# One equality table of 256 columns for both direct slots of a routed expert layer

## The chip, the cores and the metric

The kernel runs on one core of a Trainium2 chip. The metric is the device time of one launch in microseconds, lower is better. The engines are TensorE (PE: matrix products), VectorE (DVE), ScalarE (ACT), GpSimd (POOL) and SyncE (SP, which here only issues DMAs). Each runs its own list of instructions in order, and semaphores tie the lists together.

## The reference, cut to what matters

Attention (two sequences, 8 heads), then a soft expert layer, then a layer in which every one of 1536 tokens goes to its two best of eight experts. The change lies in the last of these:

```python
noisy_logits = x @ w_gate + np.log1p(np.exp(x @ w_noise)) * noise
top2 = np.argpartition(-noisy_logits, 2, axis=1)[:, :2]
top2_l = np.take_along_axis(noisy_logits, top2, axis=1)
top2_l = top2_l - top2_l.max(-1, keepdims=True)
top2_w = np.exp(top2_l)
top2_w /= top2_w.sum(-1, keepdims=True) + 1e-09
for e in range(E):
    for k in range(2):
        mask = top2[:, k] == e
        h = np.maximum(x[mask] @ w1[e], 0.0)
        out[mask] += top2_w[mask, k, None] * (h @ w2[e])
```

## The kernel before

It has three stages in one program: attention (to about 106 us of the profile), the soft expert layer, whose eight experts' weights stream in until about 141 us, and the routed layer, called the second experts here. The output of the soft layer is never written out per token: a token's row is a combination `c` of 32 slot outputs, so for the routed layer a token is 32 numbers, split in two fp16 parts and laid out as 128 columns of `crow` (line 633).

*Routing.* With the logits of all tokens in 12 groups of 128, VectorE finds each token's two best experts (lines 936 to 940), forms a mask, and TensorE counts by products with triangular matrices (952 to 959) where in its expert a token stands. From the running position `plc` come a slot number and a row inside the slot: a slot is a block of 128 tokens of one expert. Each expert owns 3 slots (`OWN`), 24 slots in all, and one further slot shares the overflow.

*Slots.* A slot is worked on in three steps: its tokens' columns are brought to `ct` (128 columns by 128 tokens), `slot_h` (line 1103) multiplies them with the expert's first weights `Gst` (already combined with the soft layer's outputs) and ScalarE and VectorE (`slot_l`, 1118) leave the rectified result in two fp16 parts, and `slot_y` (1208) makes the 24 products with the second weights `w2hl`, high part first. The result is scaled and added to the output by an indirect DMA.

*Where the columns come from.* For slots 2 and on from DRAM: GpSimd completes `crow` by the gates (`gates_a`, 1145), SyncE writes it to the DRAM table `ctab` (1152), and GpSimd gathers 128 rows per slot (`slot_a`, 1250) by the indices `gidx`, which TensorE sums out of one-hot tables (`ids`, 1198); TensorE transposes them (`slot_t`, 1012). That takes long, so slots 0 and 1, both of expert 0, go directly: `placed` (1137) compares, for each of the 12 groups, the token's key with 128 places and so writes an equality table `z` of 128 columns, and `direct` (1125) sums the products of `crow` with it, 12 products per slot. Slot 0 has its own table and so does slot 1, with all keys shifted by 2. 

*The second weights.* Expert by expert ("rank" in the code, class `Rank`, 771) fp32 weights are loaded, their largest value gives a power of two (`pow2_a` on TensorE, 753, `pow2_b` on VectorE, 760), and they are split in a high part (`w_hi`, ScalarE) and a remainder (`w_lo`, VectorE, line 811). `K0`, `K1`, `K2` are the first three ranks.

*What sets the order.* From the routed layer on, the order on PE, DVE, ACT and POOL is written out by hand: what is written first is issued first. `warm(k)` issues k products whose results nobody reads; `next(y0)` issues two of the 24 products of slot 0. SyncE restarts the weight loads only when it has read a flag `go` that GpSimd sets behind the first two gathers (1404, 1405).

*Helper tables.* `exp24`, `rows6` and `slot6` are constants, spread out by one copy each (line 929): the first by ScalarE, the other two by GpSimd.

The two lines that the change turns around most, as they were:

```python
        for t, a, by in ((exp24, K24, nc.scalar.copy), (rows6, 361, nc.gpsimd.tensor_copy), (slot6, KSLOT, nc.gpsimd.tensor_copy)):
        ...
            for t in range(a, b):
                nc.vector.tensor_scalar(z[:, t], places, keys[:, k, t:t + 1], None, ALU.is_equal)
```

Of the kernel before, what the change touches and what calls it, by code (L numbers as in the profile page):

```python
# [19 lines left out]
NT = 12  # L20
# [32 lines left out]
KSLOT = 489  # L53
# [6 lines left out]
def emit(tc, d, near=True, stop=None):  # L60
    nc = tc.nc
    es = ExitStack()
    with es:
# [696 lines left out]
        def pow2_b(px, a, b):  # L760
# [10 lines left out]
        class Rank:  # L771
# [20 lines left out]
            def w_pow_b(self):  # L792
                (self.sw, self.iw), = pow2_b(self.pw, 1, 2)
# [133 lines left out]
        for t, a, by in ((exp24, K24, nc.scalar.copy), (rows6, 361, nc.gpsimd.tensor_copy), (slot6, KSLOT, nc.gpsimd.tensor_copy)):  # L927
            n, m = t.shape[1], t.shape[2]
            by(t, k16[:, a:a + n].unsqueeze(2).to_broadcast([128, n, m]))
        K0.w_abs(0)  # L930
        K0.g_pow_a()
        warm(12)
# [27 lines left out]
        warm(3)  # L960
# [4 lines left out]
        K0.w_abs(3)  # L965
        pst = ph_([128, 2, 256]), ps_y.tile([128, 2, 256], F32, name="y")
# [158 lines left out]
        def direct(z):  # L1125
            pct = pm_([128, 128])
            for t in range(NT):
                nc.tensor.matmul(pct, crow[:, t, 0:128], z[:, t], start=(t == 0),
                                 stop=(t == NT - 1))
            return pct  # L1130

        def direct_t(pct):
            ct = wk3.tile([128, 128], F16, name="ct")
            nc.vector.tensor_copy(ct, pct)
            return ct

        def placed(z, k, a, b):
            for t in range(a, b):
                nc.vector.tensor_scalar(z[:, t], places, keys[:, k, t:t + 1], None, ALU.is_equal)

        places = k16[:, 361:489]
# [3 lines left out]
        def gates_a():  # L1145
# [6 lines left out]
            nc.sync.dma_start(out=ctab.rearrange("(p t) c -> p t c", p=128), in_=crow.bitcast(F32))  # L1152

        z0, z1 = [scratch([128, NT, 128], F16) for _ in range(2)]
        placed(z0, 0, 0, NT)
        K0.w_scale_a()
        pct0 = direct(z0)
        K0.w_pow_a()
        ttt(e2, m8[:, :, 1], m8[:, :, 0], ALU.subtract)
        nc.scalar.activation(e2, e2, AF.Exp)  # L1160
        nc.gpsimd.tensor_scalar(gts[:, 0], e2, 1.0, 1e-9, ALU.add, ALU.add)
        nc.vector.tensor_reduce(cnt8, pcnt.rearrange("p (e t) -> p e t", e=8), AX.X, ALU.add)
        t0 = direct_t(pct0)
# [11 lines left out]
        placed(z1, 1, 0, NT)  # L1175
# [6 lines left out]
        pct1 = direct(z1)  # L1182
        K1.g_scale_a()
# [3 lines left out]
        t = direct_t(pct1)  # L1187
        slot_l(*h0, (0,))
# [19 lines left out]
        def slot_y(j, hh):  # L1208
# [16 lines left out]
            ys = ((z0, z1)[j].rearrange("p t c -> p (t c)")[:, 0:1024].bitcast(F32) if j < 2 else wk3.tile([128, 512], F32, name="ys", bufs=2) if j % 3 else  # L1225
# [449 lines left out]
```

## Time and profile before

| | |
|---|---|
| time, median of 3 runs (lowest to highest) | 342.07 us (340.68 to 342.35) |
| the profiled execution's own time | 341.8 us |
| its span | 340.0 us |
| TensorE busy | 315.6 us, 93% of the span |
| VectorE, ScalarE, GpSimd busy | 200.3, 207.9, 139.5 us |
| mean granted TensorE clock | 0.98 |
| moved by DMA | 89.22 MB, 262 GB/s over the span |

The span is what the profiler saw, from the first to the last instruction; the time lies 1.8 us above it. The chain of work that ended last is of no help here, since it breaks off at the last branch of the program; the stretches of time and the waits of each engine are read instead. Names in the profile are those of tiles: most small tiles of the routing lie in one buffer and so are called `w2hl`, `k` is the table of constants, `c` on TensorE's reading side is `crow` or a constant, and `h`, `y`, `m`, `pg` are PSUM buffers. A timeline row merges neighbours that look alike and gives their number as xN, with the time from the first start to the last end.

### The profile page before, as it was taken

The numbers are of one execution on the slowest core, as the hardware profiler recorded it, in microseconds if no ns is written. First come the engines' busy times: TensorE is split into PE (matmuls) and PEld (weight loads), VectorE is DVE, ScalarE is ACT, GpSimd is POOL, SyncE is SP. The second block draws the span as 40 slices with busy tenths as digits, with TensorE's granted clock in tenths as the row PEclk, the third lists the DMA queues.
The fourth block names the chain that finished last, engine by engine and source line by source line (L and its number), as shares of the span: only waits on it lengthen the run. The fifth ranks groups of instructions, "written<-read, shape, count | busy, mean of one in ns | idle before, by whom it ended". The sixth has DMA issues, their size and how long they took to land. (4 is left out here: it accounts for less than half of the span.)

```text
span 340.0 us, 7478 instructions
## 1 busy us (share of the span) xinstructions
PE 315.6 (93%) x2691; PEld 187.7 (55%) x2691; DVE 200.3 (59%) x715; ACT 207.9 (61%) x489; POOL 139.5 (41%) x194
## 2 busy tenths in 40 slices
PE   8999999999978899977889999999999999999990
PEld 3789878888855444334554454545454545544540
DVE  2755655556526200089877685797669396898110
ACT  2788868777822211096658787496878695876320
POOL 4366543645610000122155583554653535533131
PEclk9999999999979999998799999999999999999998
DMA  6999999999999999999917999949999955222542
GB/s 178 295 329 290 316 315 313 310 271 344 339 398 400 396 394 394 393 400 393 377 33 159 300 321 362 318 105 322 299 301 291 326 179 72 35 33 32 63 63 38
DMA packets 49291, 89.22 MB, mean 262 GB/s; under 512 B 3408, under 2 KB 18384, under 8 KB 49248
## 3 DMA queue, kind: packets, MB, share of 16 engines
q1 hardware_dynamic: 44848, 81.20, 71.7%
q0 software_dynamic: 4400, 7.48, 14.1%
q8 instruction: 23, 0.38, 0.4%
q14 instruction: 20, 0.16, 0.2%
HBM read 78.53 MB, written 10.14 MB: 261 GB/s over the span
## 5 line engine op out<-in xcount | busy, mean ns | idle before, releaser
L1219 PE MATMUL y<-w2hl,hh 128*128 128x512 f16 x552 | 125.3, 379 | 0.8 <-ACT w2hl L1230 0.8
L1219 PEld LDWEIGHTS <-hh 128*128 128x128 f16 x552 | 52.5, 98 | 62.0 <-issue 4.0
L216 ACT ACTIVATE Tt<-Tt,nm 128x167 f32<-128x167 f32 x96 | 40.5, 424 | 12.9 <-DVE nm L209 12.0
L1120 DVE SCALAR_TENSOR_TENSOR hh<-h,hh 128x512 f16<-128x512 f32 x46 | 29.6, 685 | 23.0 <-ACT hh L1112 22.9
L1234 POOL DMA_INDIRECT out_y<-ys,sidx x15 | 26.9, 1794 | 27.2 <-ACT ys L1228 14.1
L811 DVE SCALAR_TENSOR_TENSOR w2hl<-w,pm,w2hl 128x1024 f16<-128x1024 f32 x28 | 35.0, 1279 | 1.2 <-issue 0.7
L231 POOL TENSOR_TENSOR Pb<-Tt,r 128x668 f32<-128x668 f32 x24 | 31.2, 1299 | 9.4 <-DVE r L223 9.1
L209 DVE CUSTOM_DVE_ANT_0 Tt<-s,bias 128x167 f32<-128x167 f32 x96 | 26.3, 328 | 14.1 <-PE s L206 14.0
L1252 POOL DMA_INDIRECT cT<-ctab,gidx x25 | 30.3, 1214 | 8.5 <-issue 4.9
L1112 ACT ACTIVATE hh<-h 128x512 f16<-128x512 f32 x46 | 25.0, 597 | 14.0 <-PE h L1111 14.0
L206 PE MATMUL s<-kx,qd 128*128 128x167 f32 x192 | 31.6, 307 | 0.4 <-DVE nm L209 0.2
L808 ACT ACTIVATE w2hl<-w,pm 128x1024 f16<-128x1024 f32 x28 | 31.4, 1150 | 0.0
L243 ACT ACTIVATE PT<-pt 128x512 f32<-128x512 f32 (+1 forms) x48 | 24.4, 558 | 10.4 <-PE pt L241 10.1
L779 ACT ACTIVATE w2hl<-w 128x1024 f16<-128x1024 f32 x28 | 29.5, 1057 | 1.7 <-DMA w<-in_w2b 1.7
L206 PEld LDWEIGHTS s<-kx,qd 128*128 128x128 f32 x192 | 28.0, 196 | 1.1 <-issue 0.6
L1234 POOL DMA_INDIRECT out_y<-c,sidx x7 | 12.2, 1739 | 37.7 <-ACT hh L1112 9.4
L241 PE MATMUL pt<-c,Pb 128*128 128x128 f32 x176 | 24.4, 280 | 1.1 <-POOL Pb L233 1.0
L257 PE MATMUL px<-PT,vt 128*64 128x128 f32 x352 | 25.4, 286 | 0.0
L241 PEld LDWEIGHTS pt<-c,Pb 128*128 128x128 f32 x176 | 18.9, 141 | 6.9 <-issue 3.0
L257 PEld LDWEIGHTS px<-PT,vt 128*64 128x64 f32 x352 | 19.5, 140 | 4.4 <-issue 3.6
L1228 ACT ACTIVATE ys<-y,gsc 128x512 f32<-128x512 f32 x15 | 10.3, 687 | 12.8 <-PE y L1219 12.8
L216 ACT ACTIVATION_READ_ACCUMULATOR Tt<-Tt,nm 128x1 f32 x96 | 17.9, 187 | 0.0
(294 smaller groups left out, 466.0 us busy)
## 6 DMA issues: line engine op xcount, KB each, us to landing
w<-in_w2b SPq DMA_DIRECT2D x14, 1024.0 KB, 12.7
x<-in_w1b SPq DMA_DIRECT2D x12, 1024.0 KB, 13.8
w<-in_w1a SPq DMA_DIRECT2D x16, 512.0 KB, 8.8
w<-in_w2a SPq DMA_DIRECT2D x16, 512.0 KB, 9.2
w<-in_w1a SPq DMA_DIRECT2D x8, 1024.0 KB, 12.1
w<-in_w2a SPq DMA_DIRECT2D x8, 1024.0 KB, 13.8
kx<-in_ka SPq DMA_DIRECT2D x12, 272.0 KB, 7.5
qd<-in_qt SPq DMA_DIRECT2D x24, 128.0 KB, 8.0
```

Of the source, the lines that this page charges most:

```text
L206: nc.tensor.matmul(s[:, t, :], qv[:, p, t, :], kx[:, p, a:a + 167], start=True, stop=True)
L216: nc.scalar.activation(Tt[:, k], Tt[:, k], AF.Exp, bias=nm[:, k:k + 1], scale=-1.0, accum_out=st[:, k:k + 1])
L231: nc.gpsimd.tensor_tensor(wide(Pn, 33, 264 + 64, 528, 167), Pu.rearrange("p (a t) c -> p a t c", t=2), rb(167), ALU.mult)
L241: nc.tensor.transpose(pt[:, ch, t], Pn[:, 2 * (n % 2) + t, 136 * ch:136 * ch + 128], ident)
L257: nc.tensor.matmul(px[64 * h:64 * h + 64, p, :], vv[:, c:c + 64], PT[:, ch, :, 64 * h:64 * h + 64], start=(ch == 0 or m == 0), stop=(ch == 1))
L779: nc.scalar.activation(w2hl[:, self.r, 1, 2 * q:2 * q + 2], self.quarter(q), AF.Abs, accum_out=self.wm[:, q:q + 1])
L808: nc.scalar.activation(w2hl[:, self.r, 0, 2 * q:2 * q + 2], self.quarter(q), AF.Copy, scale=self.sw)
L811: nc.vector.scalar_tensor_tensor(w2hl[:, self.r, 1, 2 * q:2 * q + 2], self.quarter(q), self.sw, w2hl[:, self.r, 0, 2 * q:2 * q + 2], ALU.m ...
L1120: nc.vector.scalar_tensor_tensor(hh[:, 1, 4 * q:4 * q + 4], phs[q], 0.0, hh[:, 0, 4 * q:4 * q + 4], ALU.max, ALU.subtract)
L1219: nc.tensor.matmul(py, hh[:, hx, f], w2hl[:, e, wx, f], start=(n == 0), stop=(n == 23))
L1234: o = nc.gpsimd.indirect_dma_start(out=out, out_offset=bass.IndirectOffsetOnAxis(ap=sidx[:, j:j + 1], axis=0), in_=ys, in_offset=None, com ...
L1252: nc.gpsimd.indirect_dma_start(out=cgf[:, place(n)], out_offset=None, in_=ctab, in_offset=bass.IndirectOffsetOnAxis(ap=gidx[:, n:n + 1], a ...
```

## The change

The constants get 128 more places (`2 - i / 128`), so one `tensor_scalar` compares a group's key with 256 places, and one chain of 12 products gives the columns of both slots at once; `direct_t` and the second set of keys are gone. `rows6` and `slot6` are spread out by ScalarE. `ctab` is written from GpSimd's queue. The two warming runs go from 12 to 18 and from 3 to 5. The power of two of rank 0 moves ahead into the table's steps, the high parts of rank 0 ahead of slot 0's rectification, rank 1's first-weight steps behind the index product, and the remainder of those is taken by VectorE (`g_lo`) instead of ScalarE and GpSimd (`g_scaled`, `g_rest`). The first products of slots 0 and 1 are dealt out in another order.

```diff
-KSLOT = 489
+KSLOT = 617
...
-        def pow2_b(px, a, b):
+        def pow2_b(px, a, b, fills=()):
...
             nc.vector.tensor_reduce(v[0], px, AX.X, ALU.max)
+            for f in fills[0:1]:
+                f()
             nc.vector.scalar_tensor_tensor(v[1], v[0], 2.0 ** -63, tops[:, a:b], ALU.max, ALU.mult)
+            for f in fills[1:]:
+                f()
...
-        for t, a, by in ((exp24, K24, nc.scalar.copy), (rows6, 361, nc.gpsimd.tensor_copy), (slot6, KSLOT, nc.gpsimd.tensor_copy)):
+
+        def table(t, a):
             n, m = t.shape[1], t.shape[2]
-            by(t, k16[:, a:a + n].unsqueeze(2).to_broadcast([128, n, m]))
+            nc.scalar.activation(t, k16[:, a:a + n].unsqueeze(2).to_broadcast([128, n, m]), AF.Copy)
+
+        table(exp24, K24)
...
-        warm(12)
+        warm(18)
...
-        warm(3)
+        warm(5)
...
         K0.w_abs(3)
+        table(rows6, 361)
...
         ttt(row16, bm, plc, ALU.subtract)
+        K0.w_scale_a()
+        K0.w_pow_a()
         K1.g_mm((0, 1))
...
-        places = k16[:, 361:489]
+        places = k16[:, 361:617]
...
-            nc.sync.dma_start(out=ctab.rearrange("(p t) c -> p t c", p=128), in_=crow.bitcast(F32))
-
-        z0, z1 = [scratch([128, NT, 128], F16) for _ in range(2)]
-        placed(z0, 0, 0, NT)
-        K0.w_scale_a()
-        pct0 = direct(z0)
-        K0.w_pow_a()
+            nc.gpsimd.dma_start(out=ctab.rearrange("(p t) c -> p t c", p=128), in_=crow.bitcast(F32))
+
+        z = scratch([128, NT, 256], F16)
+
+        def placed(a, b):
+            for t in range(a, b):
+                nc.vector.tensor_scalar(z[:, t], places, keys[:, t:t + 1], None, ALU.is_equal)
+
         ttt(e2, m8[:, :, 1], m8[:, :, 0], ALU.subtract)
         nc.scalar.activation(e2, e2, AF.Exp)
+        table(slot6, KSLOT)
+        placed(0, 4)
+        K0.w_pow_b(lambda: placed(4, 5), lambda: placed(5, 6))
+        placed(6, NT)
+        K0.w_hi(0)
+        K0.w_hi(1)
+        pct = direct(z)
...
-        t0 = direct_t(pct0)
-        K0.w_pow_b()
-        nc.vector.tensor_scalar(keys[:, 1], keys[:, 0], -2.0, None, ALU.add)
-        h0 = slot_h(0, t0, scratch([128, 2, 8, 128], F16), lambda: K0.w_hi(0))
+        t01 = scratch([128, 256], F16)
+        nc.vector.tensor_copy(t01, pct)
+        h0 = slot_h(0, t01[:, 0:128], scratch([128, 2, 8, 128], F16))
         K1.g_mm((2, 3))
-        K0.w_hi(1)
...
-        placed(z1, 1, 0, NT)
...
-        pct1 = direct(z1)
-        K1.g_scale_a()
...
-        t = direct_t(pct1)
-        slot_l(*h0, (0,))
+        slot_l(*h0)
...
-        slot_l(*h0, (1,))
...
-        next(y0)
-        next(y0)
-        K1.g_pow_a()
-        h1 = slot_h(1, t)
-        next(y0)
-        next(y0)
+        for _ in range(2):
+            next(y0)
+        h1 = slot_h(1, t01[:, 128:256])
+        for _ in range(2):
+            next(y0)
+        K1.g_scale_a()
...
-        K1.g_pow_b()
-        K1.g_hi()
-        K1.g_scaled()
-        K1.g_rest()
...
         for i in range(4):
             next(y1)
-        for i in range(4):
+        for i in range(2):
             next(y0)
         for q in range(4):
             ids(q)
-        h = slot_l(*h1)
+        K1.g_pow_a()
+        slot_l(*h1)
...
         K0.w_lo(0)
         K0.w_lo(1)
         fetch(3, 2)
+        K1.g_pow_b()
+        K1.g_hi()
+        K1.g_lo()
+        K2.g_mm()
         K1.g_out(0, pm_([128, 2, 256]))
         K1.g_out(1, ph_([128, 2, 256]))
-        K2.g_mm()
...
         c16[:, 361:489] = -i / 128
+        c16[:, 489:617] = 2 - i / 128
```

Three places of the order in which the engines get their instructions follow. First VectorE where the tables are made, before: the last line is the first of the block counts, and the second table comes after five more rows.

```order
L1000 TENSOR_TENSOR w2hl<-w2hl 128x12
L1139 TENSOR_SCALAR w2hl<-k_1621,w2hl 128x128 x12
L787 TENSOR_REDUCE wx<-wm 128x1
L1159 TENSOR_TENSOR w2hl<-w2hl 128x12
L1162 TENSOR_REDUCE w2hl<-h 128x8
L1134 CAST ct<-m 128x128
L765 TENSOR_REDUCE pm<-m 128x1
L766 SCALAR_TENSOR_TENSOR pm<-pm,tops 128x1
L767 TENSOR_SCALAR pm<-pm 128x1
L768 TENSOR_SCALAR pm<-pm 128x1
L1165 TENSOR_SCALAR w2hl<-w2hl 128x12
L1169 TENSOR_SCALAR w2hl<-w2hl 128x8
```

And the same place of VectorE with the change (line numbers are those of the changed file).

```order
L1160 TENSOR_TENSOR w2hl<-w2hl 128x12
L1158 TENSOR_SCALAR w2hl<-k_1621,w2hl 128x256 x4
L765 TENSOR_REDUCE pm<-m 128x1
L1158 TENSOR_SCALAR w2hl<-k_1621,w2hl 128x256
L768 SCALAR_TENSOR_TENSOR pm<-pm,tops 128x1
L1158 TENSOR_SCALAR w2hl<-k_1621,w2hl 128x256
L771 TENSOR_SCALAR pm<-pm 128x1
L772 TENSOR_SCALAR pm<-pm 128x1
L1158 TENSOR_SCALAR w2hl<-k_1621,w2hl 128x256 x6
L1170 TENSOR_REDUCE w2hl<-h 128x8
L1172 CAST w2hl<-m 128x256
L1175 TENSOR_SCALAR w2hl<-w2hl 128x8
```

The power-of-two steps of rank 0 (765 to 772) moved from behind the first cast into the table, and one cast stands behind all twelve wide steps.

Second VectorE behind the one-hot tables, before, up to the weight remainders of rank 0.

```order
L1009 TENSOR_TENSOR w2hl<-w2hl,rows_1622 128x768 x3
L765 TENSOR_REDUCE pm<-m 128x1
L766 SCALAR_TENSOR_TENSOR pm<-pm,tops 128x1
L767 TENSOR_SCALAR pm<-pm 128x1
L768 TENSOR_SCALAR pm<-pm 128x1
L1120 SCALAR_TENSOR_TENSOR hh<-h,hh 128x512 x2
L1398 TENSOR_SCALAR gidx<-m 128x25
L1399 COPY w2hl<-m 128x26
L811 SCALAR_TENSOR_TENSOR w2hl<-w_1990,pm,w2hl 128x1024 x2
L811 SCALAR_TENSOR_TENSOR w2hl<-w_1992,pm,w2hl 128x1024 x2
```

And the same place with the change.

```order
L1019 TENSOR_TENSOR w2hl<-w2hl,rows_1622 128x768 x3
L1130 SCALAR_TENSOR_TENSOR hh<-h,hh 128x512 x2
L1396 TENSOR_SCALAR gidx<-m 128x25
L1397 COPY w2hl<-m 128x26
L815 SCALAR_TENSOR_TENSOR w2hl<-w_1990,pm,w2hl 128x1024 x2
L765 TENSOR_REDUCE pm<-m 128x1
L768 SCALAR_TENSOR_TENSOR pm<-pm,tops 128x1
L771 TENSOR_SCALAR pm<-pm 128x1
L772 TENSOR_SCALAR pm<-pm 128x1
L833 SCALAR_TENSOR_TENSOR glo<-pg,pm,ghi 128x256
L815 SCALAR_TENSOR_TENSOR w2hl<-w_1992,pm,w2hl 128x1024 x2
```

Rank 1's power of two moved from ahead of `gidx` to between the two pairs of remainders, and its own remainder `glo` came to VectorE.

Third GpSimd around the row table, before (there the DMA of `ctab` stands on SyncE, ahead of the read of `go`).

```order
L1148 TENSOR_TENSOR w2hl<-w2hl,gts 128x192
L1150 TENSOR_TENSOR c_1692<-w2hl 128x8x12
L835 TENSOR_TENSOR glo<-w2hl,ghi 128x256
L1252 DMA cT<-ctab,gidx 128x72 x2
L1404 MEMSET go 1x1
L1252 DMA cT<-ctab,gidx 128x72 x5
```

And GpSimd with the change.

```order
L1148 TENSOR_TENSOR w2hl<-w2hl,gts 128x192
L1150 TENSOR_TENSOR c_1692<-w2hl 128x8x12
L1152 DMA ctab<-c_1692 128x864
L1254 DMA cT<-ctab,gidx 128x72 x2
L1402 MEMSET go 1x1
L1254 DMA cT<-ctab,gidx 128x72 x5
```

The row table's DMA took the place of `glo`, directly behind the gates and ahead of the gathers.

## Rows read from the trace of the kernel before

**Rows 1.** Windows: busy time (instructions) of each engine, granted clock, DMA.

```profile
core 0: us, PE busy (x) PEld busy (x) DVE busy (x) ACT busy (x) POOL busy (x), PEclk, DMA share, GB/s
...
160.00:163.00 3.00, 0.34 (x3) 0.12 (x3) 2.86 (x12) 3.00 (x7) 2.43 (x7) 0.97 1.02 405
163.00:166.00 3.00, 3.00 (x17) 2.08 (x17) 1.66 (x9) 1.09 (x2) 0.00 (x0) 0.50 1.03 392
...
176.00:180.00 4.00, 3.02 (x34) 1.52 (x26) 1.48 (x3) 0.30 (x2) 3.15 (x5) 1.00 0.11 18
...
200.00:332.00 132.00, 130.48 (x937) 65.22 (x934) 91.47 (x237) 89.53 (x145) 59.34 (x59) 1.00 0.71 189
```

**Rows 2.** TensorE's timeline: start us, length, operation, xcount, [idle before <-releaser].

```profile
147.63 2.75 PE L722 MATMUL y<-c 128*128 128x512 f16 x12
...
162.88 1.35 PE L1128 MATMUL m<-w2hl,c 128*128 128x128 f16 x11 [2.62 <-DVE lim L1186]
...
170.96 1.36 PE L1200 MATMUL m<-w2hl 128*128 128x26 f16 x24
...
177.76 0.23 PE L1015 MATMUL m<-k,cT 128*128 128x128 f16 x1 [0.97 <-DMA cT<-ctab,gidx]
```

**Rows 3.** VectorE's timeline, 145 to 178 us.

```profile
145.22 0.83 DVE L917 TENSOR_SCALAR w2hl<-w2hl 128x96 f32<-128x96 f32 x1 [1.30 <-ACT w2hl L910]
146.08 0.27 DVE L919 SCALAR_TENSOR_TENSOR w2hl<-w2hl 128x96 f32<-128x96 f32 x1
...
155.20 2.05 DVE L1139 TENSOR_SCALAR w2hl<-k,w2hl 128x128 f16<-128x128 f16 x12
...
159.74 2.83 DVE L1139 TENSOR_SCALAR w2hl<-k,w2hl 128x128 f16<-128x128 f16 x12
...
164.27 0.29 DVE L1134 CAST ct<-m 128x128 f16<-128x128 f32 x1 [1.41 <-PE m L1128]
...
165.08 0.17 DVE L1189 TENSOR_TENSOR w2hl<-w2hl 128x24 f32<-128x24 f32 x1
...
168.15 1.49 DVE L1009 TENSOR_TENSOR w2hl<-w2hl,rows 128x768 f16<-128x768 f16 x3
...
172.36 0.19 DVE L1398 TENSOR_SCALAR gidx<-m 128x25 int32<-128x25 f32 x1 [0.87 <-PE m L1200]
...
172.55 4.86 DVE L811 SCALAR_TENSOR_TENSOR w2hl<-w,pm,w2hl 128x1024 f16<-128x1024 f32 x4
```

**Rows 4.** GpSimd's timeline, 145 to 180 us.

```profile
145.16 0.83 POOL L929 COPY rows<-k 128x768 f16<-128x768 f16 x1
...
159.91 0.51 POOL L1177 TENSOR_TENSOR w2hl<-w2hl 128x192 f32<-128x192 f16 x1 [1.90 <-DVE w2hl L1174]
...
161.32 0.23 POOL L1180 TENSOR_TENSOR w2hl<-w2hl 128x24 f32<-128x24 f32 x1
...
162.43 0.39 POOL L1150 TENSOR_TENSOR c<-w2hl 128x96 f32<-128x96 f32 x1
...
173.95 2.13 POOL L1252 DMA_INDIRECT cT<-ctab,gidx  x1 [2.02 <-DVE w2hl L811]
176.38 1.88 POOL L1252 DMA_INDIRECT cT<-ctab,gidx  x1 [0.30 <-issue]
...
178.56 0.95 POOL L1252 DMA_INDIRECT cT<-ctab,gidx  x1 [0.24 <-issue]
```

**Rows 5.** SyncE's timeline, the issue of the row table.

```profile
162.85 0.34 SPq L1152 DMA_DIRECT2D ctab<-c  x1
```

**Rows 6.** From issue to landing, us: line 1152 (`ctab`), then line 1252 (first gathers).

```profile
DMA to landing us min/median/max: 10.2/10.2/10.2
...
DMA to landing us min/median/max: 2.4/6.5/9.9
```

**Rows 7.** DMA issues from 180 to 280 us: count, median us to landing.

```profile
cT<-ctab,gidx POOLq DMA_INDIRECT x19, 7.6
out_y<-ys,sidx POOLq DMA_INDIRECT x9, 8.9
```

More of the change, by code (lines that the diff above doesn't have):

```diff
@@ L790, in w_pow_a, with w_pow_b @@
                 self.pw = pow2_a(self.wx)
-            def w_pow_b(self):
-                (self.sw, self.iw), = pow2_b(self.pw, 1, 2)
+            def w_pow_b(self, *fills):
+                (self.sw, self.iw), = pow2_b(self.pw, 1, 2, fills)
             def g_pow_a(self):
@@ L998, in emit @@
         nc.vector.scalar_tensor_tensor(key16, slot16, 2.0, row16, ALU.mult, ALU.add)
-        keys = scratch([128, 2, NT], F32)
-        ttt(keys[:, 0], key16[:, 0:NT], key16[:, NT:], ALU.min)
+        keys = scratch([128, NT], F32)
+        ttt(keys, key16[:, 0:NT], key16[:, NT:], ALU.min)
         oj = scratch([128, NSLOT, 24], F16)
@@ L1125, in direct @@
         def direct(z):
-            pct = pm_([128, 128])
+            pct = pm_([128, 256])
             for t in range(NT):
-                nc.tensor.matmul(pct, crow[:, t, 0:128], z[:, t], start=(t == 0),
-                                 stop=(t == NT - 1))
-            return pct
[L1132 to L1139, printed above, removed]
-        places = k16[:, 361:489]
+                nc.tensor.matmul(pct, crow[:, t, 0:128], z[:, t], start=(t == 0), stop=(t == NT - 1))
+            return pct
+        places = k16[:, 361:617]
         gts = cs2.tile([128, 2, NT], F32, name="gts")
@@ L1224, in slot_y @@
                     yield
-            ys = ((z0, z1)[j].rearrange("p t c -> p (t c)")[:, 0:1024].bitcast(F32) if j < 2 else wk3.tile([128, 512], F32, name="ys", bufs=2) if j % 3 else
+            ys = (z.rearrange("p t c -> p (t c)")[:, 1024 * j:1024 * j + 1024].bitcast(F32) if j < 2 else wk3.tile([128, 512], F32, name="ys", bufs=2) if j % 3 else
                   cs2.tile([128, 512], F32, name="c16"))
@@ L1410, in emit @@
             slot_a(j)
+        for i in range(2):
+            next(y0)
         for i in range(4):
```

## The prediction

> **What bounds the kernel now.** I read the windows first, then TensorE, then each engine that TensorE waited for. From 200 to 332 us TensorE is busy 130.48 of 132 us at full clock [rows 1]: a faster helper gains nothing in that part, it only starts earlier or later. So the end is set by when this full part can begin, and by what TensorE loses before it. [...] The waits have names. At 162.88 us the second direct slot's products had let TensorE idle for 2.62 us, and at 177.76 us the transposition of the third slot's rows had waited 0.97 us for table rows gathered from DRAM [rows 2]. I call that moment T. It is the hinge: all TensorE work behind T is the same in both kernels, so the end moves as T moves, plus or minus what the clock does.
>
> Two things had to be there for T. First the indices: the second equality table began at 159.74 us, its product was copied at 164.27, the position chain followed at 165.08, the last one-hots at 168.15 (three of them, 1.49), the index product began on TensorE at 170.96, and `gidx` was written at 172.36 [rows 2, 3]. Second the row table `ctab`: SyncE issued it at 162.85 us [rows 5], and it landed 10.2 us later, at 173.05 [rows 6]; the stage loads issued before it stood ahead in the same queue. So the table came 0.5 us after `gidx`. The first gather then began only at 173.95 and took 2.13 us, the next 1.88, the third 0.95 [rows 4]; the first two lay beside VectorE's four weight remainders (4.86 us from 172.55), the third did not [rows 3, 4].
>
> **The change, part by part.** All sums are against the profiled execution, 341.8 us, of which 340.0 is span; the median of the runs, 342.07, lies 0.27 above it.
>
> *The tables leave GpSimd.* VectorE's first routing step took 0.83 us from 145.22, beside GpSimd's copy for `rows6` from 145.16 (also 0.83); the step of the same 96 columns right behind it took 0.27 [rows 3, 4]. The chain gains at most 0.56 us; I take 0.5. The six more warming products ahead of the mask product cost TensorE 6 x 2.75/12 = 1.4 us [rows 2] from 150.4 to 151.8, so they end as the mask is ready and delay nothing; were the mask earlier still, they would. On ScalarE the two copies lie ahead of evictions that nobody waits for yet; I cost them at nothing, and without that cover at about GpSimd's price, 0.83.
>
> *One table of 256 columns.* Twelve steps of 128 columns took 2.05 us, 0.17 each, and 2.83 beside GpSimd's sums [rows 3]. Twelve of 256 take no less than the 2.05, and no more than both tables together, 4.9. I take 2.4, near the lower end, since a step of only 24 columns took 0.17 too [rows 3]: much of a short step is not its columns. The second table's 2.83 us go from the path.
>
> [...]
>
> *Where the indices come out.* The keys come 0.5 us earlier, less 0.2 for two small steps moved ahead of the table, so the table starts at 154.9 instead of 155.20. Plus 2.4; plus 0.6 for the power-of-two steps now inside it (an estimate: with others they filled the 2.5 us between the two tables [rows 3]); plus 0.8 for the last product and the wider copy: both slots' columns stand at 158.7 instead of 164.27. GpSimd's sums gain little: the block counts stand behind the wide table, about 1 us, so they start at 159.7 instead of 159.91 [rows 4]. The position chain needs the last of these sums, 161.55 before [rows 4], 161.4 now, and so starts 3.7 us earlier than 165.08. The one-hots then end near 165.6. TensorE has less queued ahead of the index product (4 products between it and the second slot's first 8, where it was 8), so `gidx` comes at about 167.2, 5.2 us earlier.
>
> *The row table.* GpSimd finishes the gates at 162.6 instead of 162.82 [rows 4] and issues the DMA itself. The issue has no row: SyncE's took 0.34 [rows 5], a gather's 0.95 to 2.13 [rows 4]. Behind it on GpSimd stand only the gathers, which wait for it anyway. What decides is the landing. Gathers from this queue landed in 2.4 to 9.9 us, median 6.5 [rows 6]; from 180 to 280 us, with weight loads about, the median was 7.6, and 8.9 for the 256 KB of an output slot [rows 7]. `ctab` has 432 KB. I take 9.2 us, so 171.9, nearest the output slots; the bounds are 6.5 (169.2) and its own old 10.2 (172.9), and what lies beyond is a rival. So the table, not the indices, ends last.
>
> *T itself.* The remainders now follow `gidx` at 167.3, and steps of the next weight rank part them, so the last two run at about 170.9 to 173.3. The gather still meets them: from landing to T took 177.76 - 173.05 = 4.7 us; I take 3.9, as the last remainder ends while the first gather is being written. T is 175.8, 1.9 us earlier. SyncE's restart behind the second gather moves with it.
>
> *What the clock takes back.* By my count TensorE has done its filler by 172.6: it is the same filler, sooner done. It then idles for 3.2 us before T. Before, 2.62 us of idleness ended in a stretch at 0.50, and 0.97 us did not [rows 1, 2]. Three microseconds at half speed cost 1.5 us of work; part may fall into the wait, and small later waits may absorb some. I take half, 0.75. Sum: 341.8 - 1.9 + 0.75 = 340.65, and 0.27 up to the median: **340.9**.
>
> **The rivals.**
> *Early table.* If GpSimd's queue is served in 6.5 us or less, the gather starts before the last two remainders and is short. T is near 173.4, TensorE hardly waits, the clock stays full: 4.4 us earlier, 337.7. For it: the median of the first gathers. Against: those beside loads took 7.6, and each moved a twelfth of the bytes. Chance 0.2.
> *The clock stays full.* My sum without the 0.75: 340.2. For it: filler may run slower than I count, which shortens the wait. Chance 0.24.
> *The queue changes nothing.* The table lands near 173 as before, as the same DMA engines move it beside the same bytes; T gains 1 to 2 us from remainders already done, and the clock takes that back: 341.6, and at most 342.4. For it: beside loads GpSimd's transfers take longer, 7.6 against a best of 2.4 [rows 6, 7]. Chance 0.12.
> [...]
> *Slower: the table starves.* 256 KB took 8.9 us beside loads; scaled by 432/256 that is 15 us. It decides from a landing of about 175.2 on, 12.5 us after issue, when T, 2.5 us later as the third gather's length allows, passes the old 177.76. At 14 us: landing 176.7, T 179.2, 1.4 us late, TensorE idle for over 6 us and 1.5 us lost to the clock: 345.0. For it: the size. Against: the loads ahead are the last ones of their batch, and from 176 to 180 us the DMA engines were busy 0.11 [rows 1], so nothing feeds the starving for long. Chance 0.14.
> My own forecast keeps 0.3.
>
> **Numbers.** 0.5%, 1.7 us, is about what a measurement of this kernel can tell from no change: 340.4 to 343.8. Faster: early table and full clock, 0.44. Same: my forecast and the unchanged queue, 0.42. Slower: 0.14. The range reaches down to the early table, 337.6, and up past the unchanged queue (342.4) by a table at its slow price (1.2 us on top), 343.6; it leaves out the starving table and what lies below the early one. The forecast's own range is 340.2 to 342.1.
>
> **What would show it.** Right: TensorE no longer idle near 160 us; `gidx` near 167; the row table's landing as the last thing before the first gather; a wait of 2 to 3 us ahead of T, near 176; a granted 0.50 behind it. Wrong: `gidx` behind the table; a landing before 169 or after 175; no clock loss after the wait; over 0.3 us per step of 256 columns; or new waits of TensorE behind T, which I take to be unchanged.

## The result, and the profile after

| | before | with the change |
|---|---|---|
| time, median of 7 runs (lowest to highest) | 342.07 us (340.68 to 344.23) | 338.07 us (336.80 to 339.79) |
| the profiled execution's own time, its span | 341.8, 340.0 us | 339.79, 337.8 us |
| TensorE busy | 315.6 us | 316.5 us |
| VectorE, ScalarE, GpSimd busy | 200.3, 207.9, 139.5 us | 197.8, 208.0, 136.9 us |

The ratio of the two is 0.9889, with a 95% interval of 0.9852 to 0.9926: the change made the kernel 1.1% faster, about 4.0 us. The prediction named "faster" as the likelier side and its wide range, 337.6 to 343.6, held the time. Its own number, 340.9, was 2.8 us too high, and the forecast's own range, 340.2 to 342.1, did not hold the time. What came nearest is its first rival, the early table, which it gave 337.7 us and a chance of 0.2.

The two profiled executions differ ahead of the change, where both programs do the same work. So moments are counted from one instruction that both have: VectorE's copy of the soft layer's slot outputs (`soT`). Its timeline row before:

```profile
142.76 0.29 DVE L727 COPY soT<-m 128x128 f32<-128x128 f32 x1 [4.89 <-PE m L726]
```

And with the change, 2.74 us later:

```profile
145.50 0.29 DVE L727 COPY soT<-m 128x128 f32<-128x128 f32 x1 [4.89 <-PE m L726]
```

So the times of the two profiled executions differ by only 2.0 us: 3.9 at T and 0.9 behind it, less these 2.74 ahead.

T, the transposition of the third slot's rows, was at 177.76 - 142.76 = 35.0 us after `soT` [rows 2]. TensorE's timeline with the change has it at 176.59 - 145.50 = 31.1 us, 3.9 us earlier:

```profile
158.83 1.83 PE L1138 MATMUL m<-w2hl,c 128*128 128x256 f16 x9
161.18 0.61 PE L1121 MATMUL h<-w2hl,Gst 128*128 128x128 f16 x8 [0.52 <-DVE w2hl L1172]
...
167.90 1.36 PE L1202 MATMUL m<-w2hl 128*128 128x26 f16 x24
...
173.84 1.93 PE L652 MATMUL pg<-w2hl,soT 128*32 128x256 f32 x32 [1.70 <-issue]
...
176.59 0.22 PE L1025 MATMUL m<-k,cT 128*128 128x128 f16 x1
```

The wait of 2.62 us at the second slot's products is gone, and no wait stands ahead of T. A new one of 1.70 us stands 2.75 us ahead of it, at line 652: the product of rank 2 into `pg`, a single PSUM buffer that rank 1 must first leave (the row names no releaser; that the wait is for `pg` is shown below by b2_pow_first, where it goes). The windows with the change, in the columns of [rows 1]:

```profile
160.00:163.00 3.00, 2.48 (x30) 1.29 (x29) 2.69 (x13) 2.72 (x5) 0.70 (x2) 1.00 1.05 386
163.00:166.00 3.00, 2.83 (x20) 1.33 (x19) 2.56 (x11) 3.00 (x7) 2.36 (x7) 1.00 1.03 412
172.00:176.00 4.00, 2.30 (x36) 1.40 (x36) 3.39 (x8) 0.47 (x1) 2.88 (x3) 1.00 0.52 182
```

TensorE is busy 2.48 of 3 us where it was 0.34, and the clock stays at full speed, 1.00, where it was 0.50 behind the idleness. VectorE's timeline shows why:

```profile
147.96 0.21 DVE L921 TENSOR_SCALAR w2hl<-w2hl 128x96 f32<-128x96 f32 x1 [1.30 <-ACT w2hl L914]
148.20 0.26 DVE L923 SCALAR_TENSOR_TENSOR w2hl<-w2hl 128x96 f32<-128x96 f32 x1
...
157.50 0.88 DVE L1158 TENSOR_SCALAR w2hl<-k,w2hl 128x256 f16<-128x256 f16 x4
...
159.09 1.25 DVE L1158 TENSOR_SCALAR w2hl<-k,w2hl 128x256 f16<-128x256 f16 x6
...
160.71 0.43 DVE L1172 CAST w2hl<-m 128x256 f16<-128x256 f32 x1 [0.19 <-PE m L1138]
...
169.42 0.17 DVE L1396 TENSOR_SCALAR gidx<-m 128x25 int32<-128x25 f32 x1
...
169.60 2.47 DVE L815 SCALAR_TENSOR_TENSOR w2hl<-w,pm,w2hl 128x1024 f16<-128x1024 f32 x2
171.99 0.28 DVE L765 TENSOR_REDUCE pm<-m 128x1 f32<-128x128 f32 x1
...
173.25 0.48 DVE L833 SCALAR_TENSOR_TENSOR glo<-pg,pm,ghi 128x256 f16<-128x256 f32 x1 [0.54 <-ACT ghi L830]
```

The columns of both slots are cast 15.2 us after `soT`, where the second slot's were at 164.27 - 142.76 = 21.5 [rows 3]. The step that writes `gidx` starts at 23.9, where it started at 29.6. Behind it stand two remainders, rank 1's power of two and `glo`, and only then is `pg` free, at 173.7. GpSimd's timeline has the row table:

```profile
162.22 0.51 POOL L1182 TENSOR_TENSOR w2hl<-w2hl 128x192 f32<-128x192 f16 x1 [3.31 <-DVE lim L1189]
...
165.54 0.80 POOL L1152 DMA_DIRECT2D ctab<-c  x1 [0.33 <-POOL c L1150]
172.66 1.05 POOL L1254 DMA_INDIRECT cT<-ctab,gidx  x1 [6.32 <-DVE pm L771]
174.01 1.74 POOL L1254 DMA_INDIRECT cT<-ctab,gidx  x1 [0.30 <-issue]
```

It is issued 20.0 us after `soT`, as before (162.85 - 142.76 = 20.1) [rows 5], but it lands sooner. From issue to landing, of line 1152:

```profile
DMA to landing us min/median/max: 6.2/6.2/6.2
```

That is 6.2 us instead of 10.2 [rows 6], and the first gather starts 27.2 us after `soT` instead of 31.2 [rows 4]. The DMA view by queues (packets, MB, share of the 16 DMA engines) shows how. From 169 to 171.8 us the table's 0.44 MB run in GpSimd's queue (q0):

```profile
q0 software_dynamic: 80, 0.44, 38.6%
```

And from 172 to 174 us, with the table landed, SyncE's queue (q1) still moves stage loads, the last of which was issued by 160.74 us, ahead of the table at 165.54:

```profile
q1 hardware_dynamic: 283, 0.56, 75.0%
```

So with the change the table overtakes loads that were issued before it. Before, table and loads share q1: from 163 to 173.2 us it moves 2.82 MB, and q0 moves nothing.

One profile of the next section, that of b2_pow_first, is of a disturbed execution; of its row only the moments up to T and the waits ahead of T are used.

### The profile page after: what moved, and what is told of

Read it like the earlier page. It is cut to its first block, busy times and chain, and to the rows that moved or that the text cites. A ratio compares the mean times of both kernels' runs of the same rounds, so it can differ in the third digit from the quotient of the medians.

```text
span 337.8 us, 7453 instructions
## 1 busy us (share of the span) xinstructions
PE 316.5 (94%) x2687; PEld 187.2 (55%) x2687; DVE 197.8 (59%) x702; ACT 208.0 (62%) x490; POOL 136.9 (41%) x192
## 5 line engine op out<-in xcount | busy, mean ns | idle before, releaser
L1130 DVE SCALAR_TENSOR_TENSOR hh<-h,hh 128x512 f16<-128x512 f32 x46 | 29.6, 684 | 22.3 <-ACT hh L1122 22.3
L231 POOL TENSOR_TENSOR Pb<-Tt,r 128x668 f32<-128x668 f32 x24 | 31.2, 1300 | 9.4 <-DVE r L223 9.1
L209 DVE CUSTOM_DVE_ANT_0 Tt<-s,bias 128x167 f32<-128x167 f32 x96 | 26.3, 329 | 14.3 <-PE s L206 14.2
L1254 POOL DMA_INDIRECT cT<-ctab,gidx x25 | 28.4, 1137 | 12.8 <-DVE pm L771 6.3
L812 ACT ACTIVATE w2hl<-w,pm 128x1024 f16<-128x1024 f32 x28 | 31.3, 1150 | 0.5 <-DVE pm L771 0.5
L243 ACT ACTIVATE PT<-pt 128x512 f32<-128x512 f32 (+1 forms) x48 | 24.4, 558 | 10.4 <-PE pt L241 10.2
L241 PE MATMUL pt<-c,Pb 128*128 128x128 f32 x176 | 24.4, 280 | 1.1 <-POOL Pb L233 1.0
L257 PE MATMUL px<-PT,vt 128*64 128x128 f32 x352 | 24.5, 279 | 0.0
L257 PEld LDWEIGHTS px<-PT,vt 128*64 128x64 f32 x352 | 18.8, 136 | 4.3 <-issue 3.3
L652 PE MATMUL h<-w,siT 128*32 128x256 f32 x256 | 17.4, 418 | 1.6 <-DMA w<-in_w1a 1.5
```

The source lines that it names most:

```text
L231: nc.gpsimd.tensor_tensor(wide(Pn, 33, 264 + 64, 528, 167), Pu.rearrange("p (a t) c -> p a t c", t=2), rb(167), ALU.mult)
L241: nc.tensor.transpose(pt[:, ch, t], Pn[:, 2 * (n % 2) + t, 136 * ch:136 * ch + 128], ident)
L257: nc.tensor.matmul(px[64 * h:64 * h + 64, p, :], vv[:, c:c + 64], PT[:, ch, :, 64 * h:64 * h + 64], start=(ch == 0 or m == 0), stop=(ch == 1))
L812: nc.scalar.activation(w2hl[:, self.r, 0, 2 * q:2 * q + 2], self.quarter(q), AF.Copy, scale=self.sw)
L1130: nc.vector.scalar_tensor_tensor(hh[:, 1, 4 * q:4 * q + 4], phs[q], 0.0, hh[:, 0, 4 * q:4 * q + 4], ALU.max, ALU.subtract)
L1254: nc.gpsimd.indirect_dma_start(out=cgf[:, place(n)], out_offset=None, in_=ctab, in_offset=bass.IndirectOffsetOnAxis(ap=gidx[:, n:n + 1], a ...
```

## The experiments

Moments in us after `soT`, from each kernel's timelines; "to end" is from T to TensorE's last end. The ratio is to the kernel before on the same chip, with its 95% interval. The experiments ran on three chips: u1, a1, u4 and u2 on one, r1 and b1 to b3 on another, u5, u3, n1 and n2 on a third.

| kernel | `gidx` done | table issued | first gather | T | TensorE waits at `pg`, at T | to end | ratio |
|---|---|---|---|---|---|---|---|
| before | 29.8 | 20.1 | 31.2 | 35.0 | 0, 0.97 | 154.0 | 1 |
| the change | 24.1 | 20.0 | 27.2 | 31.1 | 1.70, 0 | 153.1 | 0.9889 (0.9852 to 0.9926) |
| r1_change_again | 24.1 | 20.1 | 27.2 | 31.1 | 1.70, 0 | 154.6 | 0.9854 (0.9789 to 0.9918) |
| u1_sync_queue | 24.3 | 19.9 | 31.4 | 34.0 | 1.71, 2.59 | 154.5 | 0.9998 (0.9964 to 1.0033) |
| a1_queue_alone | 29.9 | 20.5 | 30.2 | 34.1 | 0, 0 | 154.7 | 0.9995 (0.9961 to 1.0030) |
| u4_two_tables | 27.7 | 19.4 | 28.0 | 34.7 | 1.59, 0 | 156.6 | 1.0087 (1.0051 to 1.0122) |
| u2_pool_tables | 24.5 | 20.4 | 27.6 | 31.4 | 1.72, 0 | 154.7 | 0.9923 (0.9883 to 0.9963) |
| u5_half_steps | 25.7 | 21.6 | 28.8 | 32.7 | 1.69, 0 | 153.4 | 0.9916 (0.9881 to 0.9952) |
| u3_warm | 24.1 | 20.0 | 27.3 | 31.1 | 1.70, 0 | 153.3 | 0.9855 (0.9794 to 0.9916) |
| b1_early_gates | 24.1 | 16.1 | 24.3 | 31.1 | 1.59, 0 | 156.8 | 0.9982 (0.9944 to 1.0019) |
| b2_pow_first | 24.1 | 20.0 | 27.1 | 30.0 | 0, 0.52 | not used | 0.9854 (0.9802 to 0.9907) |
| b3_both | 24.1 | 16.1 | 24.3 | 29.6 | 0, 0.09 | 156.6 | 0.9853 (0.9800 to 0.9905) |
| n1_no_zeros | 24.1 | 16.1 | 24.4 | 29.8 | 0, 0.21 | 152.4 | 0.9803 (0.9755 to 0.9850) |
| n2_zeros_later | 24.1 | 16.1 | 24.4 | 29.8 | 0, 0.19 | 152.4 | 0.9801 (0.9746 to 0.9855) |

**u1_sync_queue**, the change with the row table's DMA back on SyncE:

```diff
-            nc.gpsimd.dma_start(out=ctab.rearrange(...), in_=crow.bitcast(F32))
+            nc.sync.dma_start(out=ctab.rearrange(...), in_=crow.bitcast(F32))
```

> The changed kernel with one line undone: the row table is issued by SyncE again, behind the stage loads. All moments are counted from VectorE's copy of soT (the third slot's transposition T stood at 35.0 us before, 31.1 us with the change). Theory A, the row table decides: it lands some 30.3 us after that copy (10 us after issue) instead of 26.3, the first gather starts near 31.2, T comes at 34.3 to 35, and the time goes back by 3 to 4 us, to 341 to 342; TensorE then waits 3 to 4 us ahead of T, and whether the granted clock falls behind that wait shows if my price for it was real. Theory B, the earlier indices and TensorE's own chain decide: T stays within 1 us of 31.1 and the time within 1 us of 338.1.

Measured: 342.22 us beside 342.16, the whole gain gone. Its timeline, SyncE, GpSimd and TensorE:

```profile
165.70 0.43 SPq L1152 DMA_DIRECT2D ctab<-c  x1
...
177.18 1.19 POOL L1254 DMA_INDIRECT cT<-ctab,gidx  x1 [11.51 <-DVE wx L791]
...
179.81 0.23 PE L1025 MATMUL m<-k,cT 128*128 128x128 f16 x1 [2.59 <-DMA cT<-ctab,gidx]
```

From the issue to the first gather it is 11.5 us, against 172.66 - 165.54 = 7.1 with the change. T then waits 2.59 us, and the window right behind it runs at half clock, as the prediction had argued from the wait of 2.62 us before:

```profile
180.20:183.50 3.30, 3.30 (x13) 1.35 (x11) 0.00 (x0) 0.15 (x1) 2.59 (x3) 0.50 0.55 122
```

**a1_queue_alone**, the kernel before with only the opposite edit, its row table on GpSimd's queue.

> The kernel before with one line changed: the row table is issued by GpSimd. Theory A in its pure form (landing alone decides): the table lands 6 us after issue, 26.3 us after the copy of soT instead of 30.3, and the time falls by 3 to 4 us, to 338 to 339. My combined reading: the indices, 29.8 us after the copy, then come last, so the gather starts near 30 and T comes near 34, 1 us earlier: 341. Theory B: no gain, 342 within 0.5.

Measured: 341.31 us, no gain that shows. GpSimd's timeline:

```profile
163.09 0.80 POOL L1152 DMA_DIRECT2D ctab<-c  x1 [0.33 <-POOL c L1150]
...
172.82 1.91 POOL L1252 DMA_INDIRECT cT<-ctab,gidx  x1 [1.12 <-DVE w2hl L1399]
```

The first gather now starts on the late indices, right behind VectorE's line 1399, 0.3 us after `gidx` is done. T is 0.9 us earlier, and in this trace the stretch behind T is 0.7 us longer. So the queue is worth nothing that shows without early indices, and early indices are worth nothing that shows without the queue.

**u4_two_tables**, the change with two tables of 128 columns and two products again, the second behind the block counts:

```diff
-                nc.vector.tensor_scalar(z[:, t], places, keys[:, t:t + 1], None, ALU.is_equal)
+                nc.vector.tensor_scalar(z01[i][:, t], places[:, 128 * i:128 * i + 128], keys[:, t:t + 1], None, ALU.is_equal)
...
+        placed(0, NT, 1)
...
+        pct1 = direct(z01[1])
```

> The changed kernel with the one part undone that its name carries: two equality tables of 128 columns, the second made and multiplied after the block counts, everything else as changed. Theory A (landing alone): the table still lands about 26.3 us after the copy of soT, the time stays within 1 us of 338.1. Theory B: the indices go back by 3 to 5 us, the gathers wait for them, and the time goes back by 3 to 4 us. My combined reading: indices at 27 to 29.5, T at 33 to 34, 2 to 3 us lost, 340 to 341.

Measured: 344.78 us, 0.9% slower than before: a miss. TensorE's timeline:

```profile
162.18 1.24 PE L1138 MATMUL m<-w2hl,c 128*128 128x128 f16 x11 [2.23 <-DVE lim L1192]
...
183.33 1.01 PE L1121 MATMUL h<-ct,Gst 128*128 128x128 f16 x8 [3.58 <-ACT ct L1028]
```

The old wait is back (2.23 us), the indices come at 27.7, and T at 34.7, hardly before the 35.0 of the kernel before and later than the 33 to 34 that I expected. The difference of T and `gidx` is 7.0 us here, as it is in the change (31.1 - 24.1), in u5_half_steps and in b1_early_gates. That is the step I had not seen: with the change's order VectorE frees `pg` only behind two remainders and rank 1's power of two, and TensorE's work from there to T takes 2.75 us more. The second row is another thing: a hold-up of 3.58 us behind T. It is taken up below.

**u2_pool_tables**, the change with `rows6` and `slot6` spread out by GpSimd again, at the old place.

> The changed kernel with the two helper tables copied by GpSimd again, ahead of the first routing step's end. Theory: VectorE's first step takes 0.8 us again instead of 0.21, the routing chain starts 0.5 us later, and T with it: 0.3 to 0.5 us lost, 338.4 to 338.6. Rival: the chain is covered by the warming products (they end after the mask), nothing lost, within 0.2 of 338.1.

Measured: 340.31 us beside 342.16. VectorE's second routing step takes three times its length beside GpSimd's copy, 0.78 us instead of the 0.26 with the change (the copy runs from 146.51 to 147.34 us):

```profile
146.41 0.21 DVE L921 TENSOR_SCALAR w2hl<-w2hl 128x96 f32<-128x96 f32 x1 [1.30 <-ACT w2hl L914]
146.66 0.78 DVE L923 SCALAR_TENSOR_TENSOR w2hl<-w2hl 128x96 f32<-128x96 f32 x1
```

The table starts 0.36 us later for it, and T is 0.35 us later (31.44 against 31.09). That is what the move to ScalarE is worth. The intervals of this kernel and the change overlap, so the times say no more; this execution also has a hold-up of 3.08 us behind T.

**u5_half_steps**, each step of 256 columns split in two of 128 at the same place, and one product for both slots as in the change.

> The change with each step of 256 columns split in two of 128, everything else as it is, one product for both slots: 24 steps at the 0.165 us of the kernel before instead of 12 at 0.2, so the table takes 4.4 to 4.8 us instead of 2.84 and the indices come 1.6 to 2.0 us later, at 25.7 to 26.1 us after soT, still ahead of the row table's landing at 26.3. Theory A (T waits for the landing alone): T at most 0.3 us later, 0.985 to 0.990 of the kernel before. Theory B (two bounds; VectorE's steps behind the indices free the pg buffer later): T 1.6 to 2.0 us later, 0.990 to 0.995.

Measured: T 1.6 us later and 0.9916, theory B's numbers. Twelve steps in VectorE's timeline (the change takes 1.25 us for six of 256 columns):

```profile
159.09 2.04 DVE L1159 TENSOR_SCALAR w2hl<-k,w2hl 128x128 f16<-128x128 f16 x12
```

But the row table was issued 1.6 us later too, since GpSimd's sums wait for the block counts behind the table, which I had left out. So this run's time and T do not tell the two theories apart. The next three kernels do.

**r1_change_again, b1_early_gates, b2_pow_first, b3_both.** b1 moves the gates and the row table's DMA ahead of the sums, b2 rank 1's power of two ahead of rank 0's remainders, b3 does both. The edits:

```diff
-        placed(6, NT)
+        placed(6, 8)
+        nc.vector.reciprocal(gts[:, 0], gts[:, 0])
+        placed(8, NT)
...
         pct = direct(z)
+        gates_a()
...
-        nc.vector.reciprocal(gts[:, 0], gts[:, 0])
...
-        gates_a()
...
-        K0.w_lo(0)
-        K0.w_lo(1)
-        fetch(3, 2)
         K1.g_pow_b()
         K1.g_hi()
+        K0.w_lo(0)
         K1.g_lo()
+        K0.w_lo(1)
+        fetch(3, 2)
```

> The changed kernel itself, beside the three kernels that follow, as their reference on this chip. Both theories: 0.989 of the kernel before, within 0.985 to 0.993, so about 338.2 us. T, counted from VectorE's copy of the slot outputs (soT), near 31.1 us, with TensorE's wait of 1.7 us ahead of K2's product into pg and none at T.

> Gates and the row table's DMA ahead of the sums: the reciprocal stands inside the equality table, so GpSimd issues the table some 4 us earlier (15.9 instead of 20.0 us after soT). Theory A (the row table's landing is still what T waits for): the gather starts 2 to 3 us earlier and T with it, 0.981 to 0.984 of the kernel before. Theory B (the change has two bounds at T within 0.1 us of each other, the gather's landing and TensorE's own order behind the single pg buffer): the gather starts 2 to 3 us earlier, TensorE's 1.7 us wait ahead of K2's product stays, T stays within 0.3 us of 31.1, and the time is that of the change, 0.987 to 0.991.

> Rank 1's power of two and its split ahead of rank 0's remainders, so that the pg buffer comes free about 2 us earlier; the row table as in the change. Theory A (TensorE's order behind pg alone sets T): T 1.7 us earlier, 0.983 to 0.985 of the kernel before. Theory B (two bounds): the 1.7 us wait goes from K2's product and a wait of 1.2 to 1.7 us stands ahead of T instead, T stays within 0.3 us of 31.1, and the time is that of the change, 0.987 to 0.991.

> Both edits together. Theory B (two bounds): now T moves, to 29.4 to 29.8 us after soT (TensorE's filler ends at 26.6, then 2.75 us of K2's and K1's products), 1.3 to 1.7 us earlier than the change: 0.984 of the kernel before, about 336.6 us. If only one of the two bound T, this kernel is no faster than b1_early_gates (theory A there) or b2_pow_first (theory A there).

Measured: r1 339.38, b1 342.64, b2 339.43, b3 339.13 us, beside 343.16. In b1 T behaves as theory B said: the gather starts 2.8 us earlier, and T stays at 31.1 behind the `pg` wait. In b2 that wait is gone, and T comes 1.1 us earlier, where theory A had 1.7 and theory B at most 0.3; it then waits 0.52 us for the gather. TensorE's timeline of b2_pow_first:

```profile
177.17 0.23 PE L1025 MATMUL m<-k,cT 128*128 128x128 f16 x1 [0.52 <-DMA cT<-ctab,gidx]
```

In b3 T moves to 29.6, as theory B said. So there are two bounds, but not as close to each other as I had read from the first profile. There the first gather's rows land 31.0 us after `soT` (176.49), 0.1 us ahead of T. In b2 they are there by 30.0, and so they are in u3_warm, where the gather starts at 27.33 and takes this long from issue to landing:

```profile
DMA to landing us min/median/max: 2.7/2.7/2.7
```

T is at 31.1 in both profiles of the change and in u3_warm. In the changed kernel it is thus `pg` that sets T, and the gather stands 0.1 to 1.1 us ahead of it.

The times do not follow T. b3 shows no gain over r1, the change on the same chip (the intervals are wide enough to hide the 1.5 us at T), and b1 is slower (0.9982 against 0.9854, and the intervals do not meet). In their traces it takes 156.6 and 156.8 us from T to the end, where r1 takes 154.6. TensorE's timeline of b3_both, with a wait of 2.49 us behind T:

```profile
172.62 0.23 PE L1025 MATMUL m<-k,cT 128*128 128x128 f16 x1
...
177.06 0.61 PE L1121 MATMUL h<-ct,Gst 128*128 128x128 f16 x8 [2.49 <-ACT ct L1028]
```

ScalarE's timeline of the same kernel, which TensorE waited for; its input is TensorE's line 844, whose rows end by 172.5 us:

```profile
174.79 0.60 ACT L847 ACTIVATE Gst<-m 128x512 f16<-128x512 f32 x1 [6.42 <-remote]
176.24 0.60 ACT L847 ACTIVATE Gst<-h 128x512 f16<-128x512 f32 x1 [0.85 <-remote]
```

The signal came over 2 us after TensorE's rows, and no engine's row stands behind it ("remote"). The windows show what follows: another stretch at half clock.

```profile
178.40:181.80 3.40, 3.40 (x10) 1.31 (x9) 3.01 (x9) 3.31 (x7) 0.00 (x0) 0.50 0.94 211
```

r1, the changed kernel itself, has such a hold-up in its profiled execution too, where the first profile of the same kernel has only 0.78 us:

```profile
181.45 1.89 PE L1221 MATMUL y<-w2hl,hh 128*128 128x512 f16 x8 [2.95 <-ACT w2hl L1232]
```

Behind this longer wait the clock stayed full. The window of r1:

```profile
181.40:185.00 3.60, 3.55 (x24) 1.89 (x24) 2.04 (x3) 3.60 (x6) 0.00 (x0) 1.00 0.94 213
```

What starts ahead of these hold-ups is SyncE's restart. In the change it comes 31.3 us after `soT`, 0.2 us behind T; in b1 and b3 at 28.5 and 27.9, 2.5 and 1.7 us ahead of T; before it came 1.4 us behind T. Its first DMA is 2 MB of zeros for the output rows. SyncE's timeline of b3_both:

```profile
170.88 0.59 SPq L875 DMA_DIRECT2D out_y<-w2hl  x1
171.57 4.71 SPq L667 DMA_DIRECT2D x<-in_w1b  x2
```

And the DMA view of the change from 172 to 200 us, in 40 slices of 0.7 us: for some 8 us from 178 on the engines are busy 9 tenths and move only about 190 GB/s, where the weight loads behind reach 439.

```profile
DMA  9656003069999999899999999999999999899999
GB/s 366 252 205 178 23 15 53 0 141 202 196 202 187 196 187 187 187 190 196 193 255 233 211 229 339 366 380 439 398 439 404 377 322 327 235 387 377 284 260 263
```

**n1_no_zeros and n2_zeros_later**: b3_both without the zeros, and with them behind the first two weight loads.

```diff
-        zero(ZREST, NTOK)
         for i in range(2):
             fetch(3, i)
+        zero(ZREST, NTOK)
```

> b3_both without the 2 MB of zeros that SyncE writes to the output directly behind its restart; the last 1024 tokens' rows are then not cleared before they are added to, so this kernel leaves that work out. Theory Z (the zeros hold up what runs behind T: their packets take 155 ns instead of 84, and while they ran GpSimd's queue moved nothing): the stall of 2.5 us that b3_both has behind T goes, T stays at 29.4 to 29.8 us after soT, and from T to TensorE's end it is 152.5 to 153.5 us instead of 156.6: 0.973 to 0.979 of the kernel before. Theory O (the stall has nothing to do with the zeros): it stays, 0.983 to 0.987.

> b3_both with the zeros issued behind the first two weight loads instead of ahead of them; nothing is left out. Theory Z: the burst comes some 5 us later, and the stall moves with it or is spread: from T to TensorE's end 153.1 to 155 us, 0.976 to 0.983 of the kernel before. Theory O: as b3_both, 0.983 to 0.987. Against both: the first scatter waits for later zeros and holds the gathers behind it, which would show as a wait of TensorE near 50 us after soT.

Measured: 335.44 and 334.49 us, beside 342.33. From T to the end both take 152.4 us. TensorE's timeline of n2_zeros_later, up to the same line 1121 that waited 2.49 us in b3:

```profile
171.14 0.23 PE L1025 MATMUL m<-k,cT 128*128 128x128 f16 x1 [0.19 <-DMA cT<-ctab,gidx]
171.20 1.03 PE L1222 MATMUL y<-w2hl 128*128 128x512 f16 x4
172.07 1.03 PE L1222 MATMUL y<-w2hl,hh 128*128 128x512 f16 x4
172.93 0.61 PE L1121 MATMUL h<-ct,Gst 128*128 128x128 f16 x8
```

There is no hold-up in either (n1's longest wait of TensorE from 150 to 330 us is 0.8 us), and in n2 the clock stays full in both windows behind T. The ratio of n2 is inside what theory Z expected, that of n1 just above it.

```profile
171.00:175.00 4.00, 3.86 (x26) 2.20 (x27) 1.60 (x8) 2.44 (x8) 2.96 (x4) 1.00 0.98 386
175.00:179.00 4.00, 3.23 (x23) 1.72 (x22) 3.67 (x7) 4.00 (x6) 0.00 (x0) 1.00 0.97 330
```

That it is the zeros which take back what T gains is argued, not shown. For it: the kernels that start the zeros well ahead of T, with nothing in front of them, all have a hold-up (b1 3.55, b3 2.49, u4 3.58 us), and n1 and n2 have none. Against it: n1 and n2 ran on the third chip, and b3 did not. On that chip u3 and u5 have no hold-up either, though their zeros start 0.2 us behind T, as in r1 and u2, which have one of 2.95 and 3.08 us on the other chips. So the 4.2 us between b3 and n2 from T to the end compare two chips; against u3, on their own chip, n1 and n2 gain about 1 (153.3 to 152.4). The ratios of b3 and n2 differ by 0.5%, and their intervals overlap (0.9800 to 0.9905, 0.9746 to 0.9855). What is shown on one chip is b1 beside r1: there the earlier restart came with a slower kernel. By what path a burst of DMAs would hold up TensorE's results no row shows, and I leave the cause open. n2_zeros_later leaves nothing out and is, level with n1, the fastest kernel of this study: 2.0% under the kernel before, the interval 1.5 to 2.5%.

**u3_warm**, the change with 12 and 3 warming products.

> The change with the old warming runs, 12 and 3 products instead of 18 and 5. TensorE is idle again for 1.4 and 0.5 us at 7.6 and 9.3 us after soT. Theory A (the waits there end with VectorE, which does not care): the clock may fall to 0.50 behind them, T stays within 0.3 us of 31.1, 0.985 to 0.991 of the kernel before. Theory B (the six and two products keep the clock up and that is worth something): a granted 0.50 between 9 and 20 us and T 0.5 to 1.5 us later, 0.990 to 0.994.

Measured: 338.83 us, T unchanged at 31.1. The window from 150 to 160 us shows TensorE less busy and the clock full all the same:

```profile
150.00:160.00 10.00, 7.45 (x67) 4.01 (x68) 9.06 (x60) 9.24 (x18) 1.10 (x3) 1.00 1.03 397
```

Theory A: the eight added products are worth nothing that shows. The idleness was shorter than expected, though: 0.79 and 0.53 us instead of 1.4 and 0.5. In the kernel before waits of 1.38 and 0.53 us stood there, and its window from 153 to 155 us is at 0.50; so this run does not show what the products are worth behind the longer wait.

## Why the prediction was right, and where it was wrong

- *The tables leave GpSimd.* 0.5 us, less 0.2: the equality table was to start 0.3 us earlier. It started 0.4 us earlier (12.0 instead of 12.4). The step beside GpSimd's copy fell from 0.83 [rows 3] to 0.21 us. u2 shows that this part is worth 0.35 us at T.
- *One table of 256 columns.* 2.4 us and 0.6 for the steps inside it, 3.0; it took 2.84. Six steps span 1.25 us, so a step comes every 0.2 us, and 12 x 0.2 is 2.4. With 128 columns a step came every 0.17 us (12 in 2.04, u5), so the added columns cost 0.03 us a step. No run shows the 1.2 us that the range's upper end adds for a table at a slow price: the whole table took 0.16 us less than the sum had.
- *Where the indices come out.* Both slots' columns 5.6 us earlier: measured 6.3. The position chain 3.7 earlier: 3.9. `gidx` 5.2 earlier: 5.7.
- *The row table: the step that failed.* I took 9.2 us from issue to landing, "nearest the output slots", with 6.5 and 10.2 as bounds. It took 6.2, below the lower bound. The gathers and output slots of 180 to 280 us were the wrong neighbours: they run in another stretch, beside other loads. Why `ctab` lands sooner than they do no row shows. It still landed after the indices were done, 26.3 us after `soT` against 24.1, so the table came last for the first gather, as predicted. u1 prices the queue itself: in the same kernel SyncE's queue brings the first gather 11.5 us after the issue, GpSimd's 7.1. The difference is 4.4 us, and without it nothing is left of the result (342.22 us in u1, beside 342.16 before). With the change `ctab`, issued at 165.54 us, lands at 171.8, ahead of loads issued by 160.74 that still move 0.56 MB from 172 to 174 us.
- *T.* Predicted 1.9 us earlier and bound by the table; it came 3.9 earlier and was bound by something else. It stands 7.0 us behind `gidx`, by way of rank 1's steps on VectorE and the `pg` buffer. The prediction had written that these steps now part the remainders, but counted them only for the gather, and had TensorE "done its filler by 172.6". In fact TensorE stopped at `pg`, which is part of that filler. b1, b2 and b3 show both bounds: without the `pg` wait T comes at 30.0 (b2), and with an earlier gather too at 29.6 (b3).
- *The clock.* The 3.2 us of idleness ahead of T and the 0.75 us lost to half clock did not come, since the gather came early. Where such a wait occurs, the loss is not certain: behind 2.59 us in u1 and 2.49 in b3 comes a stretch at 0.50, but behind 2.95 us in r1 the clock is 1.00.
- *Its sum.* The landing 3.0 us sooner than taken would have moved T by 3.0, to 30.0, which is where b2 has it; `pg` left 2.0 of them (31.1 instead of the predicted 33.0), and 0.75 were not lost to the clock. 340.9 - 2.0 - 0.75 = 338.2, against 338.07 measured. That it comes out so near is in part luck: from T to the end the first profile gains 0.9 us more (153.1 instead of 154.0), but r1 has 154.6, so nothing is built on that.
- *Its signs.* Of the signs of being right, TensorE's busy stretch near 160 us, `gidx` (near 167 in the time of the trace before: 166.7) and the table as the last thing before the first gather came; the wait ahead of T and the 0.50 behind it did not. Of the signs of being wrong, the missing clock loss came, and the landing stood at the edge (169 in that time).
- *The rivals.* The early table had T near 173.4, and T came at 142.76 + 31.1 = 173.9, but set by `pg`, which that rival did not name: that its number of 337.7 is so near is in part luck too. "The queue changes nothing" falls with u1. "The table starves" did not occur. That behind T nothing new would wait held for the first profile, not for r1.

## What to carry to other kernels

When two inputs of one step come within a microsecond of each other, ask what speeding up one alone is worth. Before, `gidx` was done 29.8 us after `soT` and the table landed at 30.3; the early table alone (a1) had a ratio of 0.9995, the early indices alone (u1) 0.9998: undo and apply each half alone before giving either the credit. Look at the queue of a small DMA that the critical path waits for: here the first gather came 11.5 us after the issue of the row table from the queue of the bulk loads (u1), and 7.1 from another. And when an earlier start releases a burst of transfers, look at what the burst now meets: in b1 the row table came earlier, T did not move, and the kernel was 1.3% slower than the change on the same chip. To say which transfer does it, the kernels that are compared have to run side by side on one chip, which b3 and n2 did not.

## What I had not expected of the hardware

- The same 432 KB landed in 6.2 us from GpSimd's queue and in 10.2 [rows 6] from SyncE's, with the stage loads in flight in both.
- Doubling a step's width from 128 to 256 columns raised the time from one step's start to the next's only from 0.17 us (12 in 2.04, u5) to 0.2.
- The first gather started about 0.9 us after the landing that it waited for (171.8 to 172.66 with the change, 173.05 to 173.95 before [rows 4]), so that much of the 4.7 us between landing and T is no engine's work.
- Zeros written to DRAM kept the DMA engines busy at about 190 GB/s, and a gather issued beside them landed later than one beside weight loads. The fourth gather took this long from issue to landing in the change:

```profile
DMA to landing us min/median/max: 9.9/9.9/9.9
```

and this long in n2_zeros_later, where the zeros came behind two loads:

```profile
DMA to landing us min/median/max: 6.6/6.6/6.6
```
